# A spectral mixer with a token MLP, forward and backward on one core: seven weight transposes begun in the row stage instead of eight, 16 filler matmuls moved behind the four sets, bias transposes begun late

## The chip, the cores and the metric

The kernel runs on one core of a Trainium2 chip. The metric is the device time of one execution in microseconds. Three executions of the kernel before took 355.19, 355.53 and 358.33 us, median 355.53. A profiled execution of it, with the time of each instruction and each transfer, is what the sections below read. TensorE is called PE, VectorE DVE, ScalarE ACT, GpSimd POOL. SP is SyncE: it computes nothing here and issues nearly all the transfers, strictly one behind the other.

## The reference

`x` is 2048 x 448, all in bfloat16. The reference makes two residual blocks and the gradients of all seven inputs that have one (`jax.vjp` with `grad_out`):

```python
def _A_ref(x, w_r, w_i):                  # spectral mixer
    X = rfft2(x); X = X * (w_r + 1j * w_i)
    return irfft2(X, s=(S, D)).astype(bfloat16)
def _B_ref(x, w1, b1, w2, b2):            # token MLP
    h = _layernorm(x)
    u = gelu(einsum("bsd,sf->bdf", h, w1) + b1)
    return (einsum("bdf,fs->bds", u, w2) + b2).transpose(0, 2, 1)
h  = x + _A_ref(_layernorm(x), A_w_r, A_w_i)
h2 = h + _B_ref(_layernorm(h), B_w1, B_b1, B_w2, B_b2)
```

S is 2048, D is 448, the hidden width F is 1792. The change concerns the forward half: the two-dimensional Fourier transform, the product with the spectral weights, the inverse transform, and one gradient product, W2 times `grad_out`, that is computed in their shade.

## The kernel before

The Fourier transforms are matmuls with tables of sines and cosines. The stages that the change touches, in order of time:

- **The row stage** (the loop over `t` at L867, until about 44 us in the profile). `row_a` and `row_b` transform 16 row tiles. Their results go through `defer(RESH_LAG, ...)` at L668 into the buffer `D2` (the tile `r2`, shown as `r`): eight copies from on-chip memory to on-chip memory that change the layout. In the same loop SP issues 18 loads of the spectral weights `W` (L573, tile `rW`) and a part of the weight transposes (L306).
- **The second stage** `s2_stage` (L671): four *sets*, each of three passes of small 32x32 matmuls over `D2` (`four`, L674, matmuls of L223), an eviction, the product with `W` on DVE (`w_mult`), another `four`, an eviction into `r452`, and four copies each into `D3` (tile `r3`, L697, 16 in all).
- **The inverse rows** `inv_rows` (L722): 16 rows, matmuls from `D3`, then the residual and the statistics of the layer norm on DVE and ACT (`h_consumer`). The first matmul reads `D3` as a whole, so it waits for the last of the 16 copies.
- **The u stage** (L1016): 7 x 32 matmuls with `W1`; ACT adds the bias `b1col` when it takes the sums out.

**Fillers.** `dg_gen` (L791) is a generator of 14 x 16 = 224 matmuls with 448 columns each, W2 times `grad_out`. `fill(n)` takes the next n of them. They keep PE at work where it would wait: 87 in and around the row stage, then `fill(30)` (L910), then 9 and 10 at each of the five steps of `s2_stage`, and the rest behind it. The whole is 224 whatever their places are.

**Weight transposes.** For every 16 fillers one block of `W2` is needed, transposed by the transfer itself (`load_w2T`, L301, `dma_start_transpose` at L306, 128 x 2048 elements). Five buffers take them in turn (`w2T_ring`, three in `rE`, two in `rO`). A finished block asks for the next load; from the number `CAP` on, `dg_gen` keeps these requests back in `held_w2` until the row stage is over (L907 to L909). Load n goes into the buffer of block n - 5.

**Biases.** `load_biases` (L779) loads `b1` and `b2` as rows of 128. `turn` transposes each with a transfer (L786) and casts it on POOL (L787) into the columns `b1col` and `b2col`. It is called from `fwd_mult` (L912) at the third set, `(s, j) == (2, 0)`, so its two transposes stand in SP's queue between the copies of the first set and those of the second.

**What sets the order.** The order on PE, DVE, ACT and SP is the order in which the program text issues the instructions (`manual_schedule`). SP waits at an instruction until the data for it is there, and everything behind it waits too. `evac` gives each eviction to ACT or DVE by a running count of their loads.

Of the kernel before, what the change touches and what calls it, by code (L numbers as in the profile page):

```python
# [34 lines left out]
RESH_LAG = 1.1  # L35
ML_F = 4
SIDE = 2
CAP = 8
N_FILL_F = (6, 3, 20, 3, 24, 2)
N_FILL_B = (16, 16, 30, 8, 24, 8)  # L40
INV_SD = 1.0 / float(S * D)
# [60 lines left out]
class Ring:  # L102
# [7 lines left out]
    def next(self):  # L110
        v = self.views[self.i % len(self.views)]
        self.i += 1
        Ring.release(v)
        return v
# [8 lines left out]
def kernel(  # L123
# [24 lines left out]
    ve = Meter(nc.vector, load, 1)  # L148
    gp_ = nc.gpsimd
# [12 lines left out]
    def cut(reg, off, *dims):  # L162
        n = int(np.prod(dims))
        v = reg[:, off:off + n]
        if len(dims) == 1:
            return v
        names = "abcd"[:len(dims)]
        return v.rearrange("p (" + " ".join(names) + ") -> p " + " ".join(names),
                           **{c: d for c, d in zip(names, dims)})
# [59 lines left out]
    def set_of(v, s):  # L229
        return v.rearrange("p (e a c) x k -> p e c a x k", e=2, a=4, c=2)[:, s // 2, s % 2]  # L230
# [53 lines left out]
    b1col = mem.tile([P, 16], F32, name="b1col")  # L284
    b2col = mem.tile([P, 16], F32, name="b2col")
# [6 lines left out]
    smc = mem.tile([P, 2, 16], BF16, name="smc")  # L292
# [417 lines left out]
    def w_mult(xc, w, y, conj):  # L710
        wr = w[:, :, 0:1, :].broadcast_to([P, 2, 2, DF])
        wi = w[:, :, 1:2, :].broadcast_to([P, 2, 2, DF])
        p1, p2 = (p_ring.next()[:, :, :, 0:DF] for _ in range(2))
        xc, y = xc[:, :, :, 0:DF], y[:, :, :, 0:DF]
        ve.tensor_tensor(out=p1, in0=xc, in1=wr, op=ALU.mult)
        ve.tensor_tensor(out=p2, in0=xc, in1=wi, op=ALU.mult)
        ve.tensor_tensor(out=y[:, :, 1, :], in0=p1[:, :, 0, :], in1=p2[:, :, 1, :],
                         op=(ALU.add if conj else ALU.subtract))
        ve.tensor_tensor(out=y[:, :, 0, :], in0=p1[:, :, 1, :], in1=p2[:, :, 0, :],
                         op=(ALU.subtract if conj else ALU.add))  # L720

    def inv_rows(consumer, n_fill, aTs, on_dve=(), halves_=False):  # L722
        def first(s1):
            pa = ps_ff()
            for c_ in range(2):
                for ch in range(2):
                    i = 2 * c_ + ch
                    mm(pa[0:KC, i * P:(i + 1) * P], lhsT=D3[:, s1, c_, DC * ch:DC * ch + KC],
                                     rhs=RTm[:], start=True, stop=True)
            aT = aTs.next()  # L730
            if s1 in on_dve:
                ve.tensor_copy(out=aT[0:KC].rearrange("p a b -> p (a b)"), in_=pa[0:KC, :])
            else:
                sc.copy(out=aT[0:KC].rearrange("p a b -> p (a b)"), in_=pa[0:KC, :])
            return aT

        flush()
        ahead_ = len(aTs.views) - 1
        q = [first(s1) for s1 in range(ahead_)]
        for s1 in range(NT):  # L740
            if s1 + ahead_ < NT:
                q.append(first(s1 + ahead_))
            aT = q.pop(0)
            fill(n_fill)
            py = ps_ff()
            for i in range(4):
                if halves_:
                    o = i // 2 * (D // 2)
                    mm(py[:, o:o + D // 2], lhsT=aT[0:KC, i, :], rhs=csI[0:KC, i // 2, i % 2, 0:D // 2],
                       start=(i % 2 == 0), stop=(i % 2 == 1))  # L750
                    continue
                mm(py[:, 0:D], lhsT=aT[0:KC, i, :], rhs=csI[0:KC, i // 2, i % 2, :],
                                 start=(i == 0), stop=(i == 3))
            consumer(s1, py)
# [3 lines left out]
    def fill(n):  # L758
        while n > 0 and pending:
            try:  # L760
                next(pending[0])
                n -= 1
                if row_ops:
                    row_ops.pop(0)()
            except StopIteration:
                pending.pop(0)

    def drain():
        while pending:
            fill(1)  # L770
# [8 lines left out]
    def load_biases():  # L779
        gp_.memset(smr, 0.0)  # L780
        nc.sync.dma_start(out=smr[0:NFB, 0, :], in_=B_b1.rearrange("(j p) -> j p", p=P))
        nc.sync.dma_start(out=smr[:, 1, :], in_=B_b2.rearrange("(j p) -> j p", p=P))

        def turn():
            for i, dst in ((0, b1col), (1, b2col)):
                nc.sync.dma_start_transpose(out=smc[:, i, :], in_=smr[:, i, :])  # L786
                gp_.tensor_copy(out=dst[:], in_=smc[:, i, :])  # L787
        return turn


    def dg_gen():  # L791
        for j in range(NFB):
            wT = w2Ts.pop(0)
            pg = ps_mm()
            for t in range(NT):
                mm(pg[:, 0:D], lhsT=wT[:, t, :], rhs=go_tp[:, t, :], start=(t == 0), stop=(t == NT - 1))
                if t == NT - 1:
                    evac(out=dgu[:, j, :], in_=pg[:, 0:D])
                    if w2T_ring.i >= cap[0]:
                        held_w2.append(load_w2T)  # L800
                    else:
                        load_w2T()
                yield

    cap, held_w2 = [CAP], []
    pending.append(dg_gen())
# [45 lines left out]
    for fn in rstd_of(4, 6):  # L852
        fn()
    fill(0)
    turn_biases = load_biases()
    Meter.side, Meter.every, Meter.count = [], 1, 0
    GROUPS = {0: (6, 8), 1: (8, 10), 3: (10, 12), 5: (12, 14), 7: (14, 16)}
    STATS = {0: (6, 7), 1: (8, 9), **{t: (t + 8,) for t in range(2, 8)}}
# [2 lines left out]
    for c in range(2):  # L861
        for e in range(2):
            sc.copy(out=Rp.rearrange("p (e a q b c) -> p c e a q b", e=2, c=2, q=8, a=2)[:, c, e],
                    in_=Rm[:, 64 * c + 32 * e:64 * c + 32 * e + 32].rearrange("p (q a b) -> p a q b", q=8, a=2))
# [42 lines left out]
    cap[0] = NFB  # L907
    while held_w2:
        held_w2.pop(0)()  # L909
    fill(30)  # L910

    def fwd_mult(s, j, x, y):  # L912
        if (s, j) == (2, 0):
            turn_biases()
        w_mult(x, set_of(W, s)[:, 2 * j:2 * j + 2], y, False)

    s2_stage(lambda s: set_of(Xs, s), fwd_mult, 9, 10, 0)
    sc.activation(out=warm, in_=eps_h, func=ACT.Sqrt)
    fill(24)
# [40 lines left out]
    def norm_h(t, on_act=False):  # L960
        if on_act:
            sc.activation(out=hln[:, t, :], in_=hn[:, t, :], func=ACT.Identity,
                          scale=rstd_h[:, t:t + 1], bias=nmr_h[:, t:t + 1])
        else:
            ve.tensor_scalar(out=hln[:, t, :], in0=hn[:, t, :], scalar1=nmean_h[:, t:t + 1],
                             scalar2=rstd_h[:, t:t + 1], op0=ALU.add, op1=ALU.mult)
# [4 lines left out]
    def load_w2c(i):  # L971
        w2cs[i] = w2c_ring.next()
        nc.sync.dma_start(out=w2cs[i], in_=B_w2.rearrange("(j p) s -> p j s", p=P)[:, :, 256 * i:256 * i + 256])

    for i in range(3):
        load_w2c(i)
    inv_rows(h_consumer, N_FILL_F[5], Ring(aT_ring.views + [cut(rO, 1024, 4, P)]), (3, 7, 11, 15))
    norm_h(10)
# [2 lines left out]
    rstd_of_h(3)  # L981
    for t in range(12, NT):
        norm_h(t, t == 14)
    drain()
    nc.sync.dma_start(out=h_d.rearrange("(p t) d -> p t d", t=NT), in_=hn)

# [401 lines left out]
```

## Time and profile before

| what | value |
|---|---|
| median of three executions | 355.53 us |
| profiled execution | 355.19 us |
| its span, first to last instruction | 353.4 us, so 1.8 us lie around it |
| matmul busy time, share of the span | 333.7 us, 94% |
| PE between fillers and first set (D2) | idle 1.38 us before 53.04 |
| PE in front of the inverse rows (D3) | idle 4.96 us before 87.59 |
| inverse rows, first matmul to first of the u stage | 87.59 to 105.95 us |
| u stage and after, PE without a break | 107.96 us on, 94.04 us long |
| POOL, waiting for the bias transposes | 29.1 us |

All places are microseconds from the first instruction of the span. A timeline row has a start, a duration, the engine, the line of the kernel, the operation, the tiles written and read, and how many instructions it joins; in brackets stands how long the engine was idle before it, and what ended that. For SP, the duration is the time its queue spent on issuing, not the time that the transfer took. "PEclk" is the clock that TensorE was granted, as a share of full speed.

### The profile page before, as it was taken

Reading aid. Unit: us, or ns where it says so; the run is one execution under the profiler, and the core shown is the slowest. Engines: PE = TensorE matmul, PEld = TensorE weight load, DVE = VectorE, ACT = ScalarE, POOL = GpSimd, SP = SyncE. Lnnn points to the kernel's source line nnn. Section 1 sums busy time; section 2 is a strip of 40 time slices with the busy share of each in tenths; the row PEclk is TensorE's granted clock in tenths of the full one; section 3 lists DMA queues with packets and bytes.
Section 4 is the critical chain, followed back from the end, with each engine's and each line's share of the span. In section 5 each row is a group of like instructions: output and inputs, shape, how many; then the busy total and the mean of one; then the engine's idle time right before and its main releaser. Section 6 shows DMA issues by size and latency. Waiting matters only on the chain.

```text
span 353.4 us, 7799 instructions
## 1 busy us (share of the span) xinstructions
PE 333.7 (94%) x2819; PEld 174.1 (49%) x2819; DVE 251.2 (71%) x667; ACT 196.9 (56%) x430; POOL 63.2 (18%) x219
## 2 busy tenths in 40 slices
PE   8579989984999999999999999999999999999995
PEld 3346645442654555555555555554334434455552
DVE  8996426860594788858323888877489886589994
ACT  5458534543796653532331345557568877588872
POOL 5776000010132000001000211110000000055760
PEclk9989999998799999999999999999999999999999
DMA  8999999937985999679686789765889798998985
GB/s 213 302 180 180 180 255 196 195 109 211 314 229 225 299 355 249 168 189 297 168 192 159 170 186 184 182 99 167 234 237 243 242 252 238 282 248 262 228 309 203
DMA packets 147247, 78.03 MB, mean 221 GB/s; under 512 B 95688, under 2 KB 139976, under 8 KB 147080
## 3 DMA queue, kind: packets, MB, share of 16 engines
q1 hardware_dynamic: 146920, 77.13, 86.1%
q8 instruction: 22, 0.36, 0.4%
q10 hardware_dynamic: 288, 0.39, 0.3%
q14 instruction: 17, 0.14, 0.1%
HBM read 25.71 MB, written 22.04 MB: 135 GB/s over the span
## 4 chain that ended last, share of the span: by engine, by line
PE 82%; DMA 6%; DVE 4%; SPq 3%; ACT 2%; issue 1%; POOL 0%; DVEq 0%; ACTq 0%
PE ps_mm L218 66%; PE ps_ff L218 13%; DMA rE<-in_B_w_dram 3%; PE ps_ff L223 3%; DVE rS L82 2%; DMA r<-r 2%; DMA rO<-in_B_w_dram 1%; DVE r L82 1%; SPq L306 1%; SPq L573 1%; SPq L316 1%; SPq L668 1%; ACT rX L82 1%; SPq L313 0%; DVE rA L82 0%
## 5 line engine op out<-in xcount | busy, mean ns | idle before, releaser
L218 PEld LDWEIGHTS <-r 128*128 128x128 bf16 (+2 forms) x600 | 56.6, 107 | 50.7 <-issue 9.1
L218 PEld LDWEIGHTS <-rS 128*128 128x128 bf16 (+2 forms) x496 | 40.7, 98 | 36.6 <-issue 7.3
L82 ACT CAST rO<-ps_mm 128x512 bf16<-128x512 f32 (+1 forms) x70 | 37.3, 583 | 15.9 <-PE ps_mm L218 14.5
L218 PE MATMUL ps_mm<-rD,r 128*128 128x448 bf16 x224 | 44.5, 352 | 0.0
L218 PEld LDWEIGHTS <-rst 128*128 128x128 bf16 (+1 forms) x320 | 23.5, 97 | 31.3 <-issue 14.1
L218 PE MATMUL ps_mm<-rC,rE 128*128 128x448 bf16 x144 | 32.5, 360 | 4.1 <-DMA rE<-in_B_w_dram 2.3
L218 PE MATMUL ps_mm<-rB,r 128*128 128x448 bf16 x160 | 31.2, 352 | 0.1
L82 ACT CAST r<-ps_ff 128x452 bf16<-128x452 f32 x41 | 22.7, 587 | 11.5 <-PE ps_ff L223 6.2
L218 PE MATMUL ps_mm<-rG,rst 128*128 128x512 bf16 (+1 forms) x128 | 28.5, 380 | 0.3 <-ACT rO L82 0.3
L218 PE MATMUL ps_mm<-r,rst 128*128 128x512 bf16 (+2 forms) x144 | 27.4, 345 | 0.0
L82 ACT ACTIVATE r<-ps_mm,rstd_h 128x448 bf16<-128x448 f32 x16 | 10.1, 633 | 26.8 <-PE ps_mm L218 26.8
L82 DVE SCALAR_TENSOR_TENSOR r<-ps_mm,b2col,r 128x448 bf16<-128x448 f32 x16 | 10.9, 682 | 19.9 <-PE ps_mm L218 17.0
L82 ACT ACTIVATE r<-rC 128x448 bf16<-128x448 bf16 x16 | 9.1, 572 | 26.7 <-DMA out_dram<-r 20.5
L82 ACT ACTIVATE rG<-rG 128x896 bf16<-128x896 bf16 x14 | 13.3, 950 | 15.0 <-DVE rG L82 14.7
L218 PE MATMUL ps_mm<-rE,rS 128*128 128x448 bf16 x112 | 21.5, 352 | 0.0
L218 PEld LDWEIGHTS <-rO 128*128 128x128 bf16 (+1 forms) x165 | 15.1, 98 | 12.9 <-DMA rO<-in_B_w_dram 0.9
L82 ACT CAST rS<-ps_ff 128x512 bf16<-128x512 f32 x31 | 17.9, 580 | 5.7 <-PE ps_ff L218 5.3
L218 PEld LDWEIGHTS <-rE 128*128 128x128 bf16 x144 | 13.5, 99 | 14.2 <-DMA rE<-in_B_w_dram 2.5
L218 PE MATMUL ps_ff<-csI,rAT 113*128 113x224 bf16 (+1 forms) x108 | 20.3, 313 | 0.0
L1136 POOL TENSOR_SCALAR lcol<-lcol 128x1 f32<-128x1 f32 x16 | 8.5, 529 | 64.7 <-ACT r L82 64.7
L82 ACT CAST rAT<-ps_ff 113x512 bf16<-113x512 f32 x24 | 13.8, 584 | 10.6 <-PE ps_ff L218 10.3
L82 DVE SCALAR_TENSOR_TENSOR rA<-ps_ff,rA 128x448 bf16<-128x448 f32 x16 | 9.9, 619 | 12.0 <-PE ps_ff L218 11.9
(189 smaller groups left out, 602.6 us busy)
## 6 DMA issues: line engine op xcount, KB each, us to landing
out_dram<-rO SPq DMA_DIRECT2D x34, 256.0 KB
r<-in_B_w_dram SPq DMA_DIRECT2D x5, 1024.0 KB
r<-r SPq DMA_DIRECT2D x32, 113.0 KB
rS<-in_B_w_dram SPq DMA_DIRECT2D x4, 896.0 KB
r<-r SPq DMA_DIRECT2D x12, 226.0 KB
out_dram<-rG SPq DMA_DIRECT2D x10, 256.0 KB
rO<-in_B_w_dram SPq DMA_DIRECT2D x2, 1024.0 KB
rC<-in_grad_out_dram SPq DMA_DIRECT2D x4, 448.0 KB
```

Of the source, the lines that this page charges most:

```text
L82: fn(**kw)
L218: nc.tensor.matmul(out, lhsT=lhsT, rhs=rhs, start=start, stop=stop)
L223: nc.tensor.matmul(out, lhsT=lhsT, rhs=rhs, start=start, stop=stop)
L306: nc.sync.dma_start_transpose(out=wT, in_=B_w2[j * P:(j + 1) * P, :].rearrange("f (t c) -> f t c", c=P))
L316: nc.sync.dma_start(out=go_tp[:, 4 * q:4 * q + 4, :], in_=go_tp_d[:, 4 * q:4 * q + 4, :])
L573: nc.sync.dma_start(out=d_ap if store else sb, in_=sb if store else d_ap)
L668: defer(RESH_LAG, lambda: resh[0].dma_start(out=D2[u:u + 125:4, 8 * e:8 * e + 8].rearrange("p g c k -> p (g c k)"), in_=cs.rearrange("p x ...
L1136: gp_.tensor_scalar(out=m1, in0=ms, scalar1=-1.0 / D, scalar2=None, op0=ALU.mult)
```

## The change

`CAP` falls from 8 to 7: the eighth block of `W2` (number 7) is no longer asked for in the row stage; it comes first of those kept back. `fill(30)` in front of the first set becomes `fill(14)`; the 16 matmuls come behind the fourth set instead, since the generator is emptied there. `load_biases` returns two functions. `turn`, the two transposes alone, is called behind the second of three loads of `W2` columns that follow the 16 copies on SP. `place`, the two casts, now on DVE, is called behind the last normalisation of the inverse rows.

```diff
-CAP = 8
+CAP = 7
...
         def turn():
             for i, dst in ((0, b1col), (1, b2col)):
                 nc.sync.dma_start_transpose(out=smc[:, i, :], in_=smr[:, i, :])
-                gp_.tensor_copy(out=dst[:], in_=smc[:, i, :])
-        return turn
+
+        def place():
+            for i, dst in ((0, b1col), (1, b2col)):
+                ve.tensor_copy(out=dst[:], in_=smc[:, i, :])
+        return turn, place
...
-    turn_biases = load_biases()
+    turn_biases, place_biases = load_biases()
...
-    fill(30)
+    fill(14)
 
     def fwd_mult(s, j, x, y):
-        if (s, j) == (2, 0):
-            turn_biases()
         w_mult(x, set_of(W, s)[:, 2 * j:2 * j + 2], y, False)
...
     for i in range(3):
+        if i == 2:
+            turn_biases()
         load_w2c(i)
...
         norm_h(t, t == 14)
+    place_biases()
     drain()
```

The order of the built program shows what follows from it. On SP the transpose of block 7 moves from between the copies into `D2` to behind the last of them; seven transposes now follow there instead of six. Six of them stand in front of the first four copies into `D3`, as six did before; the seventh, of block 13, stands behind these four instead of in front. The other twelve copies follow with nothing between them. On PE the 16 fillers move. On ACT and DVE one eviction of the first set goes from DVE to ACT, one of a filler block near the end from ACT to DVE.

## The prediction

> **What bounds the kernel now.** I read the page's busy times and clock, then the chain of waits, then PE's and SP's timelines from 40 to 110 us, then windows around PE's gaps.
>
> ```profile
> PE 333.7 (94%) x2819; PEld 174.1 (49%) x2819; DVE 251.2 (71%) x667; ACT 196.9 (56%) x430; POOL 63.2 (18%) x219
> ...
> PEclk9989999998799999999999999999999999999999
> ```
>
> PE is the bound, and the change adds and removes no matmul. So only two things can be won or lost: time in which PE waits, and time in which it runs at a lower clock (the 8 and 7 in the tenth and eleventh slice, 79.5 to 97 us). PE's timeline shows both places:
>
> ```profile
> 45.81 5.84 PE L218 MATMUL ps_mm<-rC,rE 128*128 128x448 bf16 x30
> 53.04 0.62 PE L223 MATMUL ps_ff<-r,Vt 32*32 32x452 bf16 x16 [1.38 <-DMA r<-rX]
> ...
> 78.30 1.31 PE L218 MATMUL ps_mm<-rC,rE 128*128 128x448 bf16 x6
> 79.44 3.19 PE L218 MATMUL ps_mm<-rC,rO 128*128 128x448 bf16 x16
> 87.59 1.50 PE L218 MATMUL ps_ff<-RTm,r 128*113 128x128 bf16 x12 [4.96 <-DMA r<-r]
> ```
>
> Thirty fillers, then 1.38 us of waiting for D2; at the end 22 fillers, then 4.96 us for D3. What D2 and D3 wait for is SP's queue:
>
> ```profile
> 43.22 1.96 SPq L306 DMA_TRANSPOSE rE<-in_B_w_dram  x1
> 45.28 0.58 SPq L668 DMA_DIRECT2D r<-r  x1
> ...
> 49.26 2.56 SPq L668 DMA_DIRECT2D r<-rX  x4
> 51.91 4.25 SPq L306 DMA_TRANSPOSE rO<-in_B_w_dram  x2
> 56.26 9.14 SPq L306 DMA_TRANSPOSE rE<-in_B_w_dram  x3
> 65.50 1.99 SPq L306 DMA_TRANSPOSE rO<-in_B_w_dram  x1
> 67.59 3.28 SPq L697 DMA_DIRECT2D r<-r  x4
> 70.93 2.41 SPq L786 DMA_TRANSPOSE smc<-rst  x2
> 73.45 9.01 SPq L697 DMA_DIRECT2D r<-r  x12
> 82.56 4.07 SPq L926 DMA_DIRECT2D r<-in_B_w_dram  x2
> ```
>
> From 43 to 82.5 us SP issues without a pause. The last D2 copies are issued by 51.82, although the row stage's last eviction ended at 44.6 (DVE's timeline). The first set's D3 copies start at 67.59, although their evictions ended by 62.4. So SP's order, not the data, decides when both buffers are whole.
>
> **Part 1, CAP.** The transpose at 43.22 leaves its place in front of the last six D2 copies: 45.28 - 43.22 = 2.06 us for each instruction behind it. D2's wait then ends at 53.04 - 2.06 = 50.98. The other transposes and the loads of W ahead of it stay put.
>
> **Part 2, fewer fillers in front.** 5.84 us / 30 = 0.195 us each. Fourteen end at 45.81 + 2.7 = 48.5, before D2 at 50.98. PE's gap grows from 1.38 to 2.4 us, but the set still starts 2.06 us earlier. The 16 matmuls that covered the wait (3.1 us) are paid behind the fourth set.
>
> **Part 3, the four sets.** From 53.04 to 78.30 they take 25.3 us; the fillers between them are as many, and a block ends at the same filler as before, so I carry this over: end at 76.2. Block 7 is now the one that arrives late. Its transpose starts at 51.91 - 2.06 = 49.85 and lands 4.40 us later (the chain has 4.40 for the first transpose behind the copies): 54.3. It is needed 11 fillers and one pass into the stage, 50.98 + 3.1 = 54.1. PE waited 0.22 for the transpose in that place before; the 0.2 is in the 25.3 already. The swapped evictions (0.6 us each) lie on engines that wait for PE in this stage: nothing, or 0.3 of either sign.
>
> **Part 4, D3.** SP has seven transposes and 16 copies behind 49.85. A transpose took (67.59 - 51.91)/6 = 2.61 us, a copy 9.01/12 = 0.75. The last copy starts at 49.85 + 7 x 2.61 + 15 x 0.75 = 79.4; its data is ready at 80.1 - 2.06 = 78.1 (ACT's last eviction). The chain gives that copy 5.39 us to its landing: 84.8, and PE follows 0.35 later at 85.1. Before it was 87.59: 2.5 us gained. That the bias pair leaves (73.45 - 70.93 = 2.5 us of SP) pays for the seventh transpose (2.6). Bounds: with the shortest transposes (2.0) the data and the fillers decide; 38 fillers x 0.197 (22 took 4.33) from 76.2 end at 83.7, gain 3.9. With the mean of three in the row from 56.26 (3.05) PE starts at 88.2, gain -0.6. I take 2.61, the mean of just these six in just this place.
>
> **Part 5, the clock.** PE's gap in front of the inverse rows shrinks from 4.96 to 85.1 - 83.7 = 1.4 us. Windows around the gaps: behind each stretch stand its length, what PE, PEld, DVE, ACT and POOL were busy in it, the clock (1.00, 0.50, 1.00), DMA share and GB/s:
>
> ```profile
> 17.00:20.40 3.40, 1.04 (x8) 0.54 (x8) 3.29 (x12) 0.58 (x1) 2.57 (x12) 1.00 1.05 180
> 20.40:23.80 3.40, 3.40 (x17) 2.05 (x16) 3.25 (x12) 2.48 (x4) 2.38 (x12) 0.50 0.52 121
> ...
> 51.10:54.50 3.40, 2.02 (x55) 1.21 (x54) 0.63 (x2) 0.70 (x3) 0.00 (x0) 1.00 0.87 264
> ```
>
> A stretch with 2.02 us of work left the clock at 1.00; one with 1.04 halved it for the next 3.4 us. After the 4.96 us gap it is 0.50 from 85.3 to 92. So the inverse rows run their first 4.4 us (87.59 to 92) at half speed. A gap of 1.4 should not cause that. The most it can return is 4.4/2 = 2.2 us. But ACT works without a pause from 92.67 to 105.7, and only its idle 1.78 and 0.28 before that can shrink; two thirds of it, since the first row still has to pass: I take 1.5, between 0.7 and 2.2.
>
> The Trainium skill ("TensorE: Matmul & The Clock Gate", section "Why this matters for your kernels") asks for no idle gaps over some 3 us. By it the first set's gap of 2.4 us is safe. The trace speaks against that comfort: the stretch 17.0 to 20.4 had no gap over 2.29 us (PE's timeline, before 19.76) and the clock fell. By the rule the sum stays at 351.2; by the row, where it decides, it is rival one's 351.7 to 352.9.
>
> **Part 6, biases.** The two transposes now stand behind 16 copies and five big loads, in front of one load of W2 columns that is used only after 148 us. SP reaches them at 79.4 + 0.7 + (96.25 - 82.56) = 93.8, and these loads kept the DMA engines full until about 104. DVE's casts (POOL's took 0.57 and 0.35) come at the end of the inverse rows, some 104 us. Behind them on DVE wait the first gelu steps, whose input ACT has only 6 us into the u stage; before that ACT needs b1col. PE needs the freed accumulators 12 us into it. Cost nothing; if the transposes landed 12 us into the u stage, PE would begin to wait. POOL's waits of 29.1 go, but nobody waits for POOL there. The loads of W1 move with SP; DMA idles from 104 to 108 (share 0.03), which covers a lag of a few us.
>
> **Sum**, against the profiled execution (355.19; 353.4 of span and 1.8 around it): 2.5 + 1.5 = 4.0, so 351.2. That execution is 0.3 under the median, which I leave out as noise.
>
> **Rivals.**
> *One: the clock falls in front of the first set.* The gap of 2.4 us leaves 1.0 us of work in a stretch of 3.4, as in 17.0 to 20.4, if it lies wholly inside one. Then 3.4 us at half speed cost up to 1.7 us of PE's work, of which the waits for DVE in the sets (0.22, 0.95) hide some: 0.5 to 1.7. Time 351.7 to 352.9. Against it: a gap split over two stretches leaves each over 1.7, and 13.5 to 17.0 (1.84) kept its clock.
> *Two: D3 no earlier.* The copies' own transfers, not SP, end last: the DMA share is 0.5 while they run, and the seventh transpose takes its share among them. D3 then lands at 87, PE waits 3.3 us and the clock halves again: gain 0 to 1.5, 353.7 to 355.2. For it: 5.39 us from issue to landing of the last copy is long for 113 KB.
> *Three, slower: transposes at their longest.* Single ones took 3.5 and 3.6 us on SP (at 35.14 and 24.71). With seven at 3.5 the last copy lands at 49.85 + 24.5 + 11.25 + 5.39 = 91.0, and block 7 comes a microsecond late: inverse rows 3.7 to 4.7 us later than before, 358.9 to 359.9. It decides from 2.93 us a transpose on, where D3 lands at 87.3 as before. Against it: the six in this place have a mean of 2.61, and even the three slow ones among them 3.05.
>
> **Numbers.** Forecast 0.57 (349.1 to 352.0), rival one 0.19, two 0.13, three 0.11. The likeliest gives 351.2. The lowest is both upper bounds, 355.19 - 3.9 - 2.2 = 349.1. The range runs from 349.0 into rival two, to 354.8: left out are rival three, a part of two and little below. A measurement of this kernel tells about 1% (3.6 us) from no change, so faster means under 352.0: nearly all of the forecast and a third of rival one, 0.62; within 1% 0.27; slower 0.11.
>
> **What will show it.** PE's first L223 matmul at 51.0 instead of 53.04, after a gap of 2.4; the fourth set's end near 76.2; 38 fillers behind it; the 12 copies in one run on SP without a pair between; the gap before the inverse rows under 2 us, and the clock at 1.00 after it; POOL's wait for the transposes gone; the u stage without a wait for b1col. I am wrong if block 7 makes PE wait over a microsecond, if the clock falls at 51 us, or if the last copy lands after 86.

## The result and the profile after

The changed kernel took 350.49 us (median of four executions, 349.41 to 351.69) against 355.36 for the kernel before (median of four, 352.67 to 358.33): ratio 0.985, 95% interval 0.981 to 0.989. Timed again later, beside other kernels, it took 352.85 against 356.89 (eight and 23 executions): 0.990, interval 0.986 to 0.993. So it is 1.0 to 1.5% faster; 351.2 was forecast. Its profiled execution took 351.69, the longest of its four, with a span of 349.9; against the profiled execution of the kernel before that is 3.5 us, and it is this difference that the lines below can account for.

PE's timeline of the changed kernel:

```profile
45.95 2.81 PE L218 MATMUL ps_mm<-rC,rE 128*128 128x448 bf16 x14
51.20 0.82 PE L223 MATMUL ps_ff<-r,Vt 32*32 32x452 bf16 x16 [2.45 <-DMA r<-rX]
...
52.35 4.80 PE L218 MATMUL ps_mm<-rC,rE 128*128 128x448 bf16 x19
...
77.39 4.34 PE L218 MATMUL ps_mm<-rC,rE 128*128 128x448 bf16 x22
81.57 3.19 PE L218 MATMUL ps_mm<-rC,rO 128*128 128x448 bf16 x16
85.73 0.85 PE L218 MATMUL ps_ff<-RTm,r 128*113 128x128 bf16 x12 [0.97 <-issue]
```

The first set starts 1.84 us earlier (51.20 for 53.04), after a gap of 2.45 us. Behind the fourth set stand 38 fillers, and the gap in front of the inverse rows has shrunk from 4.96 to 0.97 us. Their first 12 matmuls took 0.85 us; they took 1.50 before. The 19 fillers at 52.35, in contrast, took 0.25 us each instead of 0.20.

What ended the gap of 0.97 us the row doesn't name: "issue" stands where the profile shows no cause. The trace's records of single transfers fit D3: the last of its packets ends at 84.67 us, 1.1 us before the first matmul of the inverse rows. In the kernel before, where the row does name D3, it ends at 85.97, 1.6 us before. In e3, e7 and e9 below, whose rows say "issue" too, it ends 0.8 to 1.4 us before.

SP's timeline of the same execution:

```profile
43.45 0.58 SPq L668 DMA_DIRECT2D r<-r  x1
...
47.43 2.56 SPq L668 DMA_DIRECT2D r<-rX  x4
50.08 1.98 SPq L306 DMA_TRANSPOSE rE<-in_B_w_dram  x1
52.15 6.37 SPq L306 DMA_TRANSPOSE rO<-in_B_w_dram  x2
58.62 8.58 SPq L306 DMA_TRANSPOSE rE<-in_B_w_dram  x3
67.31 2.86 SPq L697 DMA_DIRECT2D r<-r  x4
70.69 2.53 SPq L306 DMA_TRANSPOSE rO<-in_B_w_dram  x1
73.33 8.46 SPq L697 DMA_DIRECT2D r<-r  x12
81.89 3.09 SPq L927 DMA_DIRECT2D r<-in_B_w_dram  x2
...
94.88 4.82 SPq L786 DMA_TRANSPOSE smc<-rst  x2
```

From 43 to 82 us SP has only one pause, of 0.5 us, in front of the transpose at 70.69. The copies into D2 are out 1.8 us earlier; the first copies into D3 start at 67.31, hardly earlier than before, and the twelve others run at 0.71 us each without a pair of transposes among them.

The windows around PE's gaps (behind each stretch its length, the busy time of PE, PEld, DVE, ACT and POOL, then the clock):

```profile
47.70:51.10 3.40, 1.06 (x6) 0.34 (x4) 0.98 (x4) 0.00 (x0) 0.00 (x0) 0.98 0.89 292
51.10:54.50 3.40, 3.29 (x55) 1.79 (x56) 2.02 (x4) 1.41 (x3) 0.00 (x0) 0.52 0.90 204
81.80:85.20 3.40, 2.96 (x16) 1.33 (x14) 0.41 (x1) 0.50 (x1) 0.00 (x0) 1.00 0.73 194
85.30:88.60 3.30, 2.64 (x25) 1.87 (x26) 0.94 (x4) 1.56 (x3) 0.10 (x1) 1.00 1.20 290
88.70:92.00 3.30, 3.30 (x31) 2.20 (x29) 2.40 (x8) 3.24 (x9) 0.65 (x4) 1.00 1.19 298
```

The clock fell once, after the longer gap in front of the first set; in front of the inverse rows, where it was 0.50 before, it stayed at 1.00. The account of the 3.5 us by places on PE's timeline:

| place | before | after | difference |
|---|---|---|---|
| first set starts | 53.04 | 51.20 | -1.84 |
| four sets, first matmul to last | 25.3 | 26.3 | +0.9 |
| inverse rows start | 87.59 | 85.73 | -1.86 |
| inverse rows to the u stage | 18.36 | 16.73 | -1.63 |
| u stage starts | 105.95 | 102.46 | -3.49 |
| from there to the end of the span | 247.5 | 247.4 | 0 |

Two gains, then: the inverse rows start 1.9 us earlier, and they run 1.6 us shorter. The second profile of the changed kernel ("The changed kernel again", below) shows the second gain in full, and only 0.4 us of the first.

### The profile page after: what moved, and what is told of

The parts are those of the page before. It is cut to its first block, busy times and chain, and to the rows that moved or that the text cites. A ratio compares the mean times of both kernels' runs of the same rounds, so it can differ in the third digit from the quotient of the medians.

```text
span 349.9 us, 7792 instructions
## 1 busy us (share of the span) xinstructions
PE 331.8 (95%) x2810; PEld 173.3 (50%) x2819; DVE 251.5 (72%) x669; ACT 196.6 (56%) x430; POOL 63.7 (18%) x217
## 4 chain that ended last, share of the span: by engine, by line
PE 78%; DMA 9%; DVE 5%; ACT 4%; SPq 2%; issue 2%; POOL 0%; DVEq 0%; ACTq 0%
PE ps_mm L218 66%; PE ps_ff L218 8%; DMA rE<-in_B_w_dram 3%; PE ps_ff L223 3%; DMA r<-in_B_w_dram 3%; DVE rS L82 2%; DMA rO<-in_B_w_dram 2%; ACT rO L82 1%; DVE r L82 1%; SPq L306 1%; DMA r<-rX 1%; DVE rA L82 1%; DMA out_dram<-rG 1%; SPq L316 1%; ACT rX L82 1%
## 5 line engine op out<-in xcount | busy, mean ns | idle before, releaser
L218 PEld LDWEIGHTS <-r 128*128 128x128 bf16 (+2 forms) x600 | 55.7, 105 | 45.9 <-issue 3.9
L218 PE MATMUL ps_mm<-rC,rE 128*128 128x448 bf16 x144 | 33.6, 371 | 4.0 <-DMA rE<-in_B_w_dram 2.5
L218 PE MATMUL ps_mm<-rG,rst 128*128 128x512 bf16 (+1 forms) x121 | 26.8, 380 | 1.1 <-issue 0.8
L218 PE MATMUL ps_ff<-csI,rAT 113*128 113x224 bf16 (+1 forms) x108 | 19.0, 298 | 0.4 <-ACT rAT L82 0.2
L218 PE MATMUL ps_mm<-rC,rO 128*128 128x448 bf16 x80 | 18.3, 353 | 0.0
```

The source lines that it names most:

```text
L218: nc.tensor.matmul(out, lhsT=lhsT, rhs=rhs, start=start, stop=stop)
```

## The experiments

The theory: SP's order decides when D2 and D3 are whole, the moved fillers close the gap in front of the inverse rows, and with that the clock stays up there. Its rivals are that one part alone makes the gain, and that the clock is worth nothing. Seven kernels and the one before make up all eight combinations of the three parts; each ratio is against executions of the kernel before made beside it.

| | CAP | fillers in front | bias transposes | median us | ratio, 95% interval |
|---|---|---|---|---|---|
| e1 | 7 | 30 | early | 357.28 | 1.003, 1.000 to 1.007 |
| e2 | 8 | 14 | early | 353.07 | 0.992, 0.989 to 0.995 |
| e3 | 8 | 30 | late | 352.24 | 0.990, 0.984 to 0.995 |
| e3 again | 8 | 30 | late | 354.71 | 0.994, 0.991 to 0.997 |
| e4 | 7 | 14 | early | 355.99 | 0.999, 0.997 to 1.002 |
| e5 | 8 | 14 | late | 353.44 | 0.993, 0.990 to 0.997 |
| e6 | 7 | 30 | late | 357.08 | 1.004, 1.001 to 1.008 |
| changed | 7 | 14 | late | 350.49 | 0.985, 0.981 to 0.989 |
| changed again | 7 | 14 | late | 352.85 | 0.990, 0.986 to 0.993 |

**e1, CAP alone.** The kernel before with:

```diff
-CAP = 8
+CAP = 7
```

> The kernel before with CAP = 7 alone: 30 fillers stay in front of the first set, the bias pair stays between the copies. My theory: D2 is whole at 51.1 instead of 53.0, but block 7 now lands at about 54.4 and the 30 fillers need it from their 25th on (at 50.6), so PE waits near 3.8 us for it and the first set starts at about 55.4, 2.4 later than before; D3 comes 2.5 later on SP (one transpose more behind D2), PE idles 5 us or more before the inverse rows and the clock halves there: 2 to 3 us slower, 357 to 358.5. Rival (the two microseconds on D2 are the gain and need no partner): 353.3, 2 us faster.

No gain, as the theory expected; by the interval, no clear loss either. PE's timeline of the profiled execution, the longest of its ten:

```profile
45.54 4.89 PE L218 MATMUL ps_mm<-rC,rE 128*128 128x448 bf16 x25
55.75 2.05 PE L218 MATMUL ps_mm<-rC,rE 128*128 128x448 bf16 x5 [5.32 <-DMA rE<-in_B_w_dram]
```

The first 25 of the 30 fillers run, then PE waits 5.32 us for block 7 (3.8 were expected), which now comes behind the D2 copies. The first set starts at 57.73.

**e6, all but the moved fillers.** The changed kernel with:

```diff
-    fill(14)
+    fill(30)
```

> The changed kernel with fill(30): CAP 7 and the late bias transposes stay. My theory: PE waits among the 30 fillers for block 7, which lands at 54.4, so the first set starts at 55.5 to 57.7, 4 to 6 us later than in the changed kernel; only 22 fillers lie behind the fourth set: 354 to 356.5. Rival (the moved fillers only trade one gap for another): 350.5 to 351.5.

The median, 357.08, lies half a microsecond above the expected range. The profile has the same wait (4.28 us before 54.58), and the late biases don't make up for it. Block 7 late and 30 fillers in front exclude each other.

**e2, the moved fillers alone.** The kernel before with:

```diff
-    fill(30)
+    fill(14)
```

> The kernel before with fill(14) alone. My theory: D2 does not move (53.0), PE idles 4.4 us before it and the clock halves in the first set (0.5 to 1.2 us lost); the 16 fillers behind the fourth set shorten the gap before the inverse rows from 5.0 to about 1.8 us, D3 as before or 1 us later, and the clock stays up there (1.4 us won): 354 to 356, no difference that a measurement can tell. Rival (the moved fillers alone are the gain): 350.5 to 352.

A miss by a microsecond: 353.07, between what the two expected, and 0.8% faster than the kernel before with one number changed. Its profiled execution was the longest of its ten (356.11): a gap of 4.26 us before the first set, two half-speed stretches there, and inverse rows of 16.74 us. So the gain of 1.6 us at the end is there; what the gap in front costs in the other executions, no profile shows.

**e3, the bias part alone.** The changed kernel with CAP = 8 and fill(30).

> The kernel before with the bias part alone (transposes behind the five big loads, casts on VectorE); CAP 8 and fill(30) stay. My theory: 2.5 us of SP leave from between the copies, but the last four copies then wait for their evictions (80.1), so the last one starts at about 80.6 instead of 81.9 and D3 lands 1.3 to 2.5 us earlier; PE's gap before the inverse rows is 2.5 to 3.7 us and the clock may still halve: 352.5 to 354.2. Rival (bias part is all of the gain): 350.5 to 351.5. Rival (bias part is worth nothing, POOL was idle anyway): 355.

PE's timeline and SP's:

```profile
84.91 1.40 PE L218 MATMUL ps_ff<-RTm,r 128*113 128x128 bf16 x12 [2.19 <-issue]
```

```profile
67.89 14.02 SPq L697 DMA_DIRECT2D r<-r  x16
```

With nothing among them, the 16 copies take 14.02 us, and the inverse rows start 2.7 us earlier than in the kernel before. After a gap of 2.19 us their clock still halves (they take 17.84 us). The second measurement was made beside the changed kernel:

> The bias part alone once more, beside the changed kernel on the same chip. If CAP and the fillers add something to it, it is 1 to 2.5 us slower than the changed kernel, 352 to 353.5. Rival (the bias part is the whole gain): as fast as the changed kernel within 0.7 us.

354.71 against 352.85: the bias part is not all of the gain; the changed kernel is 1.9 us faster beside it. Whether it is the largest part is not shown: e2's ratio lies between its two. The moved fillers alone were not timed beside the changed kernel, and e2's interval overlaps the changed kernel's second one. So how much the bias part and CAP = 7 add to the moved fillers stays open.

**e4, all but the bias part.** The kernel before with CAP = 7 and fill(14).

> The changed kernel without the bias part: CAP 7 and fill(14), the bias pair back between the copies, in the row of SP just behind the seventh transpose. My theory: first set at 51.2 as in the changed kernel, but D3 lands 2.4 us later than there, at 88, as late as in the kernel before; PE idles 3.3 us before the inverse rows and the clock may halve there: 353.5 to 356. Rival (the order on SP does not matter, the copies' own transfers end last): 350.5, as the changed kernel.

No faster than the kernel before in the median, as the theory expected. But its profiled execution, the shortest of its ten (353.50), doesn't show the reason given: there the inverse rows start at 86.41 after a gap of 0.21 us and run at full speed. What delays the others is not seen.

**e5, all but CAP.** The changed kernel with:

```diff
-CAP = 7
+CAP = 8
```

> The changed kernel with CAP = 8: fill(14) and the late bias transposes stay, the eighth transpose goes back in front of the D2 copies. My theory (D2 two microseconds earlier is what lets the sets start earlier): D2 at 53.0, gap 4.3 us, clock halves in the sets, fourth set ends at 79.4 to 80.3, 38 fillers end at 86.8 to 87.6 and are what the inverse rows then wait for, 1.1 to 1.9 us later than the changed kernel: 351.5 to 352.5. Rival (from the single parts: fill alone 0.992, bias alone 0.990, CAP alone 1.003; they add, and CAP 7 costs): 349 to 350, as fast as the changed kernel or faster.

The median is 353.44, a microsecond above what the theory expected; the rival's 349 to 350 is out. PE's timeline and windows of its profiled execution (352.47; the shortest took 352.45):

```profile
52.74 0.82 PE L223 MATMUL ps_ff<-r,Vt 32*32 32x452 bf16 x16 [3.47 <-DMA r<-rX]
...
82.97 3.19 PE L218 MATMUL ps_mm<-rC,rO 128*128 128x448 bf16 x16
86.01 0.85 PE L218 MATMUL ps_ff<-RTm,r 128*113 128x128 bf16 x12
```

```profile
48.80:52.20 3.40, 0.47 (x3) 0.03 (x1) 0.40 (x1) 0.00 (x0) 0.00 (x0) 1.00 0.94 296
52.40:55.60 3.20, 2.86 (x53) 1.63 (x54) 1.62 (x3) 1.41 (x3) 0.00 (x0) 0.50 1.00 201
```

The clock halves in the sets, as expected. Block 7 is early here, and the sets take 26.1 us instead of 25.3: the fallen clock alone costs them 0.8 us.

Here D3 is ready before the fillers are done: the late first set (52.74) now moves the end. CAP = 7 takes that away, and is worth 0.9% by the changed kernel's first measurement (0.993 to 0.985, intervals apart) and 0.4% by its second (0.993 to 0.990, intervals overlapping, so not clear of noise). The single parts don't add up: each changes which of D2, block 7, the fillers and D3 comes last.

**e8, the clock alone.** The kernel before with 24 matmuls more in the gap of 4.96 us:

```diff
     fill(24)
     drain()
+    keep_warm(24)   # 24 x matmul(ps, lhsT=ident, rhs=go_tp[:, 0, :]), read by nobody
```

> The kernel before with 24 matmuls of 448 columns more behind the fillers, in front of the inverse rows (identity and grad_out, read by nobody; about 4.5 us of PE in the gap of 4.96). It prices the clock alone: D3 comes as before, the inverse rows run at full speed from the start, 16.8 instead of 18.4 us: 1.3 to 1.7 us faster, 354.2 to 354.6 against a median of 355.9. Rival (ACT sets the pace of the inverse rows, the clock is worth nothing there): 355.9.

353.47 against 356.25, ratio 0.994 (0.991 to 0.998): 2.0 us by the ratio, 2.8 by the medians, where 1.3 to 1.7 were expected. The rival, no gain, is out. PE's timeline and the windows:

```profile
82.76 4.70 PE L809 MATMUL ps_ff<-rC,ident 128*128 128x448 bf16 x24
87.83 0.85 PE L218 MATMUL ps_ff<-RTm,r 128*113 128x128 bf16 x12 [0.37 <-DMA r<-r]
```

```profile
85.30:88.60 3.30, 2.93 (x24) 1.64 (x22) 0.00 (x0) 0.33 (x1) 0.00 (x0) 1.00 1.06 277
88.70:92.00 3.30, 3.09 (x25) 2.06 (x26) 1.93 (x6) 2.27 (x6) 0.44 (x2) 1.00 1.18 301
```

D3 comes no earlier (87.83), the clock stays at 1.00, and the inverse rows take 16.74 us instead of 18.36. That is 1.62 of the 1.63 us that the changed kernel gains there, with nothing else changed.

**e7, the clock in front of the first set.** The changed kernel with 11 such matmuls behind `fill(14)`.

> The changed kernel with 11 matmuls of 448 columns more in front of the first set (product of the identity and grad_out, into an accumulator that nobody reads; about 2.1 us of PE in the gap of 2.45). Clock theory: no half-speed window at 51 us, the sets take 25.3 instead of up to 26.3 us, and 0.5 to 1 us is won at the end: 349.4 to 350.2. Rival (the inverse rows wait for D3, so a faster set changes nothing, or the clock is not what lengthens the sets): 350.5, or 351 if the matmuls are in D2's way.

351.99 against 356.25, ratio 0.990 (0.986 to 0.994): above what either expected, and no gain on the changed kernel's 0.985 and 0.990. The windows and PE's timeline:

```profile
51.70:55.10 3.40, 3.14 (x59) 1.79 (x59) 2.29 (x5) 1.58 (x4) 0.00 (x0) 1.00 0.91 196
```

```profile
52.65 2.25 PE L218 MATMUL ps_mm<-rC,rE 128*128 128x448 bf16 x11
56.10 1.69 PE L218 MATMUL ps_mm<-rC,rE 128*128 128x448 bf16 x8 [1.20 <-DMA rE<-in_B_w_dram]
```

The clock is at 1.00, the 11 fillers take 0.20 us each, and then PE waits 1.20 us for block 7, whose transpose started at 50.63. The sets take 26.3 us, as long as in the changed kernel. There the slow fillers had hidden that block 7 is late. So beside a late block 7 the fallen clock cost nothing, while in e5, where the block is early, it cost 0.8 us: two causes stood in one place, and taking away one laid open the other.

**The changed kernel again**, beside e3 and e9:

> The changed kernel itself, timed again beside the two below, since its first figure (350.49, ratio 0.985) rests on four executions of another day than the experiments. My theory: its executions scatter with the number of half-speed clock windows, so the median may lie a microsecond higher: 350.4 to 352, ratio 0.983 to 0.989. Rival: below 350.4.

352.85: higher, as the theory said, but by 2.4 us and beyond its range of 350.4 to 352; the ratio, 0.990, lies just outside its own. Its profiled execution (353.14) had a gap of 3.67 us before the first set, at 51.60, and inverse rows from 87.20 of 16.74 us. The shorter inverse rows are there again. The earlier start is only 0.4 us (87.59 before), though the last copy into D3 was issued at 81.25, almost as early as in the first profile (81.17). Why it took 5.95 us from there to the first matmul instead of 4.56, the profile doesn't show.

**e9, D2 earlier in another way.** CAP stays 8; four of the 18 loads of W move behind the D2 copies. The changed kernel with:

```diff
-CAP = 7
+CAP = 8
...
-    W_AT = {t: 1 if t % 2 else 2 for t in range(12)}
+    W_AT = {t: 1 if t % 2 else 2 for t in range(9)}
...
-    for _ in w_loads:
-        pass
...
     gen_inv_d(1)
+    for _ in w_loads:
+        pass
     cap[0] = NFB
```

> The changed kernel with CAP = 8 and the last four loads of W issued behind the eight D2 copies instead of between them. If SP's order in front of D2 is what counts and CAP is only one way to change it: D2 is whole near 50.4 without making block 7 late, the gap in front of the first set is 1.7 us (too short to halve the clock), the sets take 25.3 us and end at 75.8, 38 fillers end at 83.2, and D3 lands at about 83, so the inverse rows start 2 to 2.5 us earlier than in the changed kernel: 348 to 349.5. Rival (the product with W waits for its last loads, or the D3 copies on SP end no earlier): 350.5 to 352.

352.12 against 356.89, ratio 0.989 (0.985 to 0.992): the changed kernel beside it had 352.85, no difference to be told. PE's timeline, then SP's:

```profile
50.65 0.62 PE L223 MATMUL ps_ff<-r,Vt 32*32 32x452 bf16 x16 [1.16 <-DMA r<-rX]
...
80.54 3.19 PE L218 MATMUL ps_mm<-rC,rO 128*128 128x448 bf16 x16
85.90 0.85 PE L218 MATMUL ps_ff<-RTm,r 128*113 128x128 bf16 x12 [2.17 <-issue]
```

```profile
49.59 2.61 SPq L573 DMA_DIRECT2D rW<-in_A_w_i_dram  x4
52.30 5.44 SPq L306 DMA_TRANSPOSE rO<-in_B_w_dram  x2
57.83 8.15 SPq L306 DMA_TRANSPOSE rE<-in_B_w_dram  x3
66.09 2.93 SPq L697 DMA_DIRECT2D r<-r  x4
69.55 2.39 SPq L306 DMA_TRANSPOSE rO<-in_B_w_dram  x1
72.06 9.67 SPq L697 DMA_DIRECT2D r<-r  x12
```

D2 is earlier as expected, the fourth set's end (76.4) and the fillers' (83.7) too. But the last copy into D3 is issued at 81.1, as in the changed kernel (81.2), so the inverse rows don't move, and the gap that the fillers leave halves the clock:

```profile
83.30:86.70 3.40, 1.23 (x15) 0.74 (x12) 0.62 (x1) 0.36 (x1) 0.00 (x0) 1.00 1.03 280
86.90:90.10 3.20, 3.12 (x12) 1.61 (x13) 1.24 (x3) 1.43 (x4) 0.23 (x1) 0.50 1.20 290
```

The rival was right: in this profile D3 comes last, and an earlier D2 is worth nothing that could be measured.

**e10, four D3 copies taken off SP.** e9 with the first set's copies issued by GpSimd:

```diff
-defer(RESH_LAG, lambda g=g, ab=ab: resh[0].dma_start(out=D3[...], in_=ab), ab)
+eng = gp_ if s == 1 and scale is None else nc.sync
+defer(RESH_LAG, lambda g=g, ab=ab, eng=eng: eng.dma_start(out=D3[...], in_=ab), ab)
```

> The kernel with the last four loads of W behind the D2 copies (CAP 8, fill(14), late biases), and in addition the first set's four copies into D3 issued from GpSimd, which is idle then, instead of SP. In that kernel the D3 copies on SP were what came last (last one issued at 81.1, inverse rows at 85.9 after a gap of 2.2 us and a half-speed window). Theory (SP's queue is what delays D3): the four copies run among the transposes from 60 us on, SP's other twelve start near 68 and the last one is bound by its eviction at 78; D3 is whole before the fillers end at 83.7, no gap over 1 us, no half-speed window: inverse rows at 83.8 to 84.3, 3 to 3.7 us won on that kernel, 348.5 to 349.5, ratio 0.977 to 0.981. Rival (the transfers themselves, on the DMA engines, end last, whoever issues them; or the copies from GpSimd slow the transposes down): no better than that kernel, 0.986 to 0.99.

352.91 against 356.14, ratio 0.991 (0.986 to 0.995): no better than e9. SP's timeline and the chain of waits (start, length, what):

```profile
57.84 12.80 SPq L306 DMA_TRANSPOSE rE<-in_B_w_dram  x3
70.75 2.90 SPq L306 DMA_TRANSPOSE rO<-in_B_w_dram  x1
73.75 10.43 SPq L698 DMA_DIRECT2D r<-r  x12
```

```profile
67.12 0.67 PE ps_ff L223 x44
67.80 2.46 issue
```

The copies themselves were issued in 2.61 us from 60.15 on, and took 9.0 us to land (median). But the three transposes beside them held SP for 12.80 us instead of 8.15, one of them alone 8.13, and PE stood 2.46 us in the middle of the third set for no reason that the profile shows. The sets took 29.5 us, and the inverse rows started at 87.52, without a gap. The four copies were off SP's queue, and the transposes took back what that freed. D3's last packet ended at 86.6 us, in e9 at 84.8. So whether D3 would come earlier with SP's queue relieved is still not shown. Whether the copies did it by their transfers or by where they were issued was not tried.

## Why the prediction was right

- **CAP, D2.** Forecast 50.98, measured 51.20 (51.60 in the second profile). Right, and for the reason given: the D2 copies behind the transpose moved by 1.8 us.
- **Fewer fillers in front.** The gap was to be 2.4 us and was 2.45.
- **The four sets.** Forecast 25.3 us, measured 26.3. The step that failed is "Part 3": block 7 was to land 4.4 us after its issue, at 54.3. In e7, where nothing hides it, PE goes on at 56.10, 5.5 us after the issue (5.2 in e1, 4.8 in e6): a wait of 1.2 where 0.2 was carried over. In the profiled execution the slow clock covered it. The forecast of the time held all the same, because the inverse rows then waited 0.97 us for D3 anyway; that was luck.
- **D3.** Forecast 85.1, measured 85.73: a gain of 1.9, not 2.5. The six transposes took (67.31 - 50.08)/6 = 2.87 us each, not 2.61. The copies took 0.71, not 0.75, and from the last one's start (81.2) to PE's went 4.6 us, not 5.7. The last copy started 1.8 us later than forecast, and the way from there was 1.2 shorter: the two errors partly cancel, which is luck too. In the second profile that way took 5.95 us, and the gain was 0.4. Transposes were the term to watch: by the forecast's own terms there is no gain from 2.96 us each on (it says 2.93).
- **The clock.** Forecast 1.5 us, measured 1.63, and e8 has the same 1.62 with nothing else changed. The gap was to be 1.4 us and was 0.97 (1.62 in the second profile). Right, and shown.
- **Rival one** was seen in the profiled execution: half speed from 51.1 to 54.5, one of the three signs that the forecast gave for being wrong. Its price of 0.5 to 1.7 us holds where block 7 is early (0.8 in e5). Added to the forecast it was wrong: e7 shows that with block 7 late the sets take as long without it.
- **Biases.** Nobody waited for them: DVE's casts took 0.17 us each at 106.85, and ACT used `b1col` at 108.50, 6.0 us into the u stage as before. POOL's wait for the transposes is gone. On SP the pair took 4.82 us, twice as long as before, in front of one load that nobody waits for.
- **The sum.** 4.0 us were forecast against the profiled execution; the profiled one after is 3.5 shorter, the medians 4.9 and 4.0.

What the prediction didn't say is how much the parts need each other. It priced them one by one; but CAP = 7 pays only with both of the others. Alone it brings nothing (e1, 1.003). Held against the same kernels with CAP = 8, it costs 0.7% with the moved fillers alone (e4's 0.999 for e2's 0.992) and 1.0 to 1.4% with the late biases alone (e6's 1.004 for e3's 0.994 and 0.990). The fillers and the late biases together, without CAP = 7, are no better (0.993) than the fillers alone (0.992).

## What to carry to other kernels

Where one queue issues everything, a transfer moved out of the way of one wait goes into the way of the next: follow the queue to the last wait behind it, and move the matmuls that cover the waits along with it. A gap in front of a dense stage costs twice, once as waiting and once as a lower clock afterwards, so a few microseconds of spare matmuls there can pay, as the 0.6% of e8 shows. Parts of such a change have to be tried in all combinations: here one part alone reached more than half of the gain, and another brought nothing or cost time unless both of the others were there.

## What the runs showed of the hardware

- **Gaps well under 3 us can halve the clock.** After a gap of 2.45 us (1.06 us of PE work in 47.7 to 51.1) the changed kernel ran 3.4 us at half speed, and so did e9 after a gap of 2.17 (1.23 us of work in 83.3 to 86.7). Gaps of 0.97 and 1.38 us did not do it. The gap's length alone doesn't decide: a gap of 2.47 us in front of e10's first set and one of 2.44 in front of e2's inverse rows left the clock at 1.00; each was split over two stretches (with 1.88 and 2.44 us of PE work in e10's, 1.96 and 2.17 in e2's). Between 10 and 95 us in the 14 profiles, every full-speed stretch with under 1.5 us of PE work was followed by half speed, and none with over 1.7. The Trainium skill ("TensorE: Matmul & The Clock Gate", "Why this matters for your kernels") asks for no gaps over about 3 us. Here the measurement decides: 2.17 us was enough.
- **Executions of the kernel before scatter with the clock.** In the traces' records of the clock, half speed lasts 3.41 us or twice that, except at the very end. From each execution's mean granted clock one can work out how many stretches of 3.41 us it ran at half speed, (1 - clock) x 2 x span / 3.41. In 25 executions of the kernel before, beside e1 to e4, the number lay between 2.1 and 5.2, and time went with it: about 352.3 us plus 0.94 us for each (correlation 0.72). That is no proof of a cause, since a longer wait both takes time and lowers the clock. In the changed kernel's eight later executions time did not go with the number (correlation -0.2). The changed kernel had 2.3 to 2.7 of them on average, the kernel before 3.9 to 4.2. The same page ("Part 1: The HAM clock gate (the "warmup" mystery)") says that the stretch runs freely and doesn't start with the kernel. The gaps of 2.45 us (nearly all in one stretch, clock halved) and 2.47 us (split, clock kept) above fit that. Single executions that differ by 1% therefore say little here.
- **A small transpose behind big loads is slow to issue.** The pair of 128 x 16 transposes held SP for 2.41 us between the D3 copies and for 4.82 us behind five loads of about a megabyte. In all the profiles it is 2.41 to 3.44 us there (five) and 4.75 to 5.02 us here (nine).
